# Decay scans with a reset row in PSUM, a dense load of w, four shared PSUM banks and a new issue table, in a gated-recurrence and spatial-gating kernel

## The chip, the cores and the metric

The kernel runs on one core of one Trainium2 chip. The metric is the device time in microseconds (us) of one execution. The time before is 393.78 us, the median of three runs (393.39 to 418.01).

## The reference

Two stages follow each other. The first is a linear recurrence per batch (4) and head (8) over 768 steps with 48 channels: a 48 x 48 state is decayed by w and gets k v^T added at each step, and r reads it together with a bonus term u*k*v^T. The second is a gated feed-forward layer whose gate mixes the 768 positions.

```python
for t in range(S):
    cur = einsum(u * k[t], v[t])
    y[t] = einsum(r[t], state + cur)
    state = w[t][:, None] * state + einsum(k[t], v[t])
h = maximum(x @ w_in, 0)            # x is y, heads side by side: 768 x 384 a batch; d_ff = 1024
u, v = halves of h                  # 512 columns each
v_n = (v - mean) / sqrt(var + 1e-6)
v_s = w_spatial @ v_n + b_spatial
out = (u * v_s) @ w_out
```

All numbers are fp32. The inputs w lie between 0.8 and 0.95.

## The kernel before

The recurrence is done in chunks of 128 steps: 4 batches x 6 chunks, 24 chunks or slots. In a slot the channels of two heads lie on 112 partitions (48, a pad of 16, 48), and four such pairs lie side by side, so that a tile is 112 x (4 x 128).

- `slot_load` (L343) issues five loads on the SyncE queue: W (decays, 129 columns a group with a leading zero), kk (k), rr (r), N (r and k with steps on partitions) and v.
- `slot_prep` (L358) first lets ScalarE check that no w exceeds 1 (L379 or L383, a Relu of w - 1 with a sum into `over`). VectorE then runs two `tensor_tensor_scan`s: L387 forms F, the products of w from a step to the end of the chunk, with the reset ones in the constant row `zr`; L368 forms the running products from the start, in place in W, with 1/Wc as reset value (L390, L392; Wc is the product over the chunk) in the constant row `zf`. kk is multiplied by F (L394) and rr by W (L396). L400 to L403 form the diagonal dg of the bonus term, and L415 (GpSimd) or L420 (ScalarE, four multiplies a tile) put it on a diagonal tile As.
- `slot_a` (L434) multiplies kk and rr on TensorE into two PSUM tiles pa, and L439 copies their upper triangles into As. `slot_kt` (L451, L455) transposes kk by way of a PSUM tile pt into KT. `slot_s` (L505 to L521) makes the state's increment pd, and the state S, Sd. `slot_y` (L470) sums the slot's output in the PSUM tile py.
- `slot_x` splits py into a rounded part and a rest (hi, lo) for three-pass matmuls: L534 casts hi on ScalarE; for the first eight slots L537 subtracts it on TensorE and L540 casts lo on ScalarE.
- `hv_unit`, `g_unit` and `out_unit` are the second stage; their matmuls (ph, pu, pv, po) stand at L547 to L549.

`split64`, `prep_sp` and their kin split the weights into hi and lo at the start, on the vector engines, between the first slots.

PSUM has 8 banks. Before, `psM` has four (tag "pm": ph, pu, pv, po and the filler tile pw), and `psA` one each for A0, A1 (the two pa), py and pt (which pd uses too).

Every piece of work is recorded as an op with the engines that may do it, and the table `PLAN` gives each op an engine and a place; `issue` emits the ops sorted by that place, so that the table alone sets the order on every engine. `fill` goes along TensorE's part of the table and puts matmuls of zeros (`warm`, L748, tile pw) where the table leaves it a gap of over 0.3, up to the sixth slot:

```python
if t < last.start and o.start - t > GAP:
    warm((o.start - t - 0.1) / (0.214 if t > first else 0.43))
```

These fillers are instructions in TensorE's stream like any other. If a value of w is over 1 or a chunk's product is too small, `range_check` sets a flag and `general` does the whole work in another way; the given inputs do not come to that.

Of the kernel before, what the change touches and what calls it, by code (L numbers as in the profile page):

```python
# [8 lines left out]
F32 = mybir.dt.float32  # L9
# [7 lines left out]
C = 128  # L17
# [11 lines left out]
T0 S1s S19u Sv6 A14s V1af V1fu V1jh A1tg V28j Snk Ax7 V2cb V2gb V2rx A2tx V2vr S1mi A1wk V2b5 V2tu V2xo A2zo  # L29
V330 S0 S3b Sb6 S53 S84 A7d V7d Vct Vdc Vim Vaw Vr8 Vdt Vfh Vh4 Af8 Aip Gm1 Ttr Vx6 Vzo Tdf Ag2 Tzt T134  # L30
A16i T18h A19o S12r A1ce V34x V36i V3ad A3ev V3o7 Sgh Aq4 V1le V1mn V1uc A20o V3tk S1x6 A2ip V3d9 V3q4 V3x1
A3z2 V40v S5mh A5tl V5xc S1jh A1s1 G5hi S1qk A1ya G5qr S1l0 A1v5 G55w S5u8 A68z G7hj S18b A1ff V7cf S5z2
A669 V7pi S595 A5v0 V706 S71v A78z V7r1 S7kh A7tx V7wz S7e5 A7le V7ny S7po A7wr V7yi S2u0 A32m V3ca V3s1
V3vi A3x6 G4dl S3cg A3m7 V5ps V64f V6db A6i9 G72o S2zr A38d V5tj V5yw V60j A62p G6ll S3z4 A4lt V71p V77k
V7aw A7eq V7kb T2c7 T31i T37h A3nm A3pw A3qk Scx Seq Srm Skj S9n An1 Vnt Vup Vz7 V11o Vv5 V18i Vt5 Gx2 V1ck
Ahj A1gu A1l6 T1b1 V1ok V1rk Ti6 Vm1 Gzw A17u A13a Txo Az9 T1r7 T1u6 T1vh A22e T24d A2dd T2fc T33g T39f A3c0
A3eb A3tu Ste Sz8 S10z S1eo S16t A10r V153 G1f5 V1tk V1zo G1bl V26m G1ok G1ri V233 A1e3 A24p A291 T295 V2i8
V2dh T11e V1bl G1hr A1zp A23q T1fv V1hr T2ku T2m5 T2ng A2s4 T2u3 A2vn T2xm T2zk T35j A39s A3gk A3h8 A3wd
G4pl V4tu V4ue G4y9 G4zi G505 V52m A55f A57s V5do A536 A5d9 V5nu A5jn A5lz V623 S1cw S1hp S217 S24r S1vn
A1pi V1w9 G2ag V2fh V2zl G233 V38f G2dh G2i8 V2l8 A2kf A2mt G2q5 T3bn V3f2 V3h3 T1k3 V1ql G2l2 A2wz A2r5  # L40
T27c A2ep T3hp T3jp T3l0 A40s T4dy A4gv T4kc T4ma T4o8 A4xm A50x A59h S28p S2c3 S2px S2mw S2rp A2g6 V2mq
V362 V3ee V3ks G3ee V3yy G3hy V42s V44g A2ys A48o G4bt T426 V4g4 V4e4 T2hk V2q5 G44c A45x A4ji T3n8 V4ce
T4ir T4qg T4rr A4vb T4xi A51h T5g7 T5i5 T5k3 A5no A5pz A5qm S3aj S3fh S3n4 S46w S3l6 A3jo V45y V4bd V4bx
V4j8 V49g V4rx G4ge V4mn V4oa A3t0 A4pv G4q5 T4ug V4y9 V532 T4er V4i5 G4o6 A4wn A4uc T53d T566 T57h A5bx
T5dw A5ib T5qt T5sr T5up A5xb A5zl A609 A644 V640 V65y G69t G6cr G6ev G6iu G6jh V6rt A6tm V75n A6o9 A6ql
V7m1 A6k7 A6mk G6v8 T6p4 T3qq T3xk T458 A47c T76b T77s T7dk T7f1 T7ot T7qs V7sw V7vf A7y6 G81m T3tk T3w4
T485 A4d0 T6py T6re T6su T798 T83v T85b V88r V8aj A8c6 V8dp T3z0 T40g T46p A4kh T71z T73f T74v T7ao T7s8
T7to V81m G84e A893 V8f8 T49l T4b1 T4ch A4i7 T6ua T6vq T6x7 T7c4 T7z1 T80h V84o V877 A8ai V8c2 T8jt T8l9
T8tz T8vf A8xi S8z0 T8o6 T8pm T8r2 T8si A8um S8xb T8fh T8gx T8id T8mq A8ot S8qb T5m1 T5zt T6fs A6sa T86r
T888 T89o T8b4 T8ck T8e0 V8gs G8j4 A8m3 V8vd T619 T62p T646 A67o T8wv T8yb T92o T9a4 T9bk Tacp Vaet Gakp  # L50
# [154 lines left out]
def kernel(  # L205
# [670 lines left out]
```

## Time and profile before

| what | us |
|---|---|
| median of three runs | 393.78 |
| the profiled execution's own time | 393.65 |
| its span, first to last instruction | 391.8 |
| around the span | 1.85 |
| TensorE busy in the span | 377.2 |
| VectorE, ScalarE, GpSimd busy | 276.8, 200.0, 142.1 |
| fillers (pw), all before 94.5 | 32.8 |
| last matmul ends | about 385.5 |

The profile is of one execution. Busy time is the union of an engine's instructions; TensorE's matmuls are pipelined, so the ends of two that follow each other overlap. An fp32 matmul (pw, pa, py, pd) shows as two records, one fp32r matmul (L547 to L549) as one. An engine's idle time is put down to what released it last.

### The profile page before, as it was taken

What the parts mean: (1) busy time and instruction counts of PE and PEld (TensorE: products, weight loads), DVE (VectorE), ACT (ScalarE), POOL (GpSimd) and SP (SyncE); (2) the same over time, 40 slices, a digit from 0 to 9 for tenths busy, and PEclk for the clock granted to TensorE, in tenths of its full rate; (3) what the DMA queues carried; (4) which work ended last, traced back from release to release, by engine and by line L of the source; (5) the groups of instructions that cost most, each with busy time, mean ns of one, the idle gap of its engine ahead of it and who ended that gap; (6) DMA issues with size and microseconds to landing.
All of it is one profiled execution on the core that took longest, in us unless ns stands there. A gap on an engine that the chain in (4) does not pass through costs nothing.

```text
span 391.8 us, 9107 instructions
## 1 busy us (share of the span) xinstructions
PE 377.2 (96%) x3638; PEld 342.4 (87%) x3638; DVE 276.8 (71%) x466; ACT 200.0 (51%) x511; POOL 142.1 (36%) x172
## 2 busy tenths in 40 slices
PE   7899989899999999999999999999999999999993
PEld 6788778788899988989988988899988899999993
DVE  5688978869878687878977978995688714414140
ACT  4477675879455457565356256574145604521211
POOL 3248406549433464534431126416343103021110
PEclk9999999999999999999999999999999999999997
DMA  7996562662332545243067434243041110001101
GB/s 233 299 311 195 164 198 64 194 195 57 100 99 84 148 119 154 93 138 96 1 176 197 114 106 135 84 127 107 2 146 40 37 62 0 2 20 40 63 2 69
DMA packets 23091, 43.79 MB, mean 112 GB/s; under 512 B 2688, under 2 KB 10496, under 8 KB 23040
## 3 DMA queue, kind: packets, MB, share of 16 engines
q1 hardware_dynamic: 23040, 43.12, 36.9%
q8 instruction: 30, 0.49, 0.5%
q14 instruction: 21, 0.17, 0.1%
HBM read 38.39 MB, written 4.72 MB: 110 GB/s over the span
## 4 chain that ended last, share of the span: by engine, by line
PE 73%; DMA 9%; DVE 8%; issue 3%; ACT 2%; POOL 2%; SPq 1%; POOLq 0%; ACTq 0%; DVEq 0%
PE pv L547 9%; PE pv L549 8%; PE pv L548 8%; PE py L470 7%; PE pa L434 4%; PE po L547 4%; PE po L549 4%; PE po L548 4%; PE pu L547 4%; PE pu L548 4%; PE pu L549 3%; PE ph L547 3%; PE ph L549 3%; PE ph L548 3%; DMA W<-in_tr_dram 3%
## 5 line engine op out<-in xcount | busy, mean ns | idle before, releaser
L547 PE MATMUL pv<-ws,vh 128*128 128x384 f32 x192 | 66.3, 345 | 0.1
L549 PE MATMUL pv<-ws,vl 128*128 128x384 f32 x192 | 64.6, 337 | 0.0
L548 PE MATMUL pv<-ws,vh 128*128 128x384 f32 x192 | 64.6, 336 | 0.0
L657 ACT CAST gh<-t 128x384 fp32r<-128x384 f32 x32 | 16.1, 510 | 55.5 <-POOL t L655 27.7
L439 DVE COPY_PREDICATED As<-mask,pa 128x512 f32<-128x512 int32 x48 | 34.0, 731 | 9.4 <-PE pa L434 4.7
L547 PEld LDWEIGHTS pv<-ws,vh 128*128 128x128 f32 x192 | 36.1, 188 | 1.9 <-issue 0.4
L415 POOL TENSOR_SCALAR_AFFINE_SELECT As<-dg 128x512 f32<-128x512 f32 x26 | 21.8, 843 | 41.3 <-DVE dg L403 26.4
L387 DVE TENSOR_TENSOR_SCAN F<-W,zr 112x516 f32<-112x516 f32 x24 | 32.2, 1343 | 6.2 <-ACT F L383 3.6
L548 PEld LDWEIGHTS pv<-ws,vh 128*128 128x128 f32 x192 | 36.1, 188 | 0.2
L549 PEld LDWEIGHTS pv<-ws,vl 128*128 128x128 f32 x192 | 36.1, 188 | 0.0
L420 ACT ACTIVATE As<-ident,dg 128x128 f32<-128x128 f32 x88 | 27.9, 391 | 14.4 <-DVE dg L403 11.6
L547 PE MATMUL pu<-xT,wi 128*128 128x384 f32 x96 | 33.8, 352 | 1.4 <-ACT ph L579 1.4
L748 PE MATMUL pw<-zr 128*128 128x128 f32 x228 | 32.8, 292 | 1.7 <-DVE zr L250 1.7
L653 DVE TENSOR_TENSOR t<-pv,b_sb 128x384 f32<-128x384 f32 x32 | 17.5, 552 | 23.6 <-PE pv L549 23.6
L547 PE MATMUL po<-wo,gh 128*128 128x384 f32 x96 | 33.0, 344 | 0.0
L748 PEld LDWEIGHTS pw<-zr 128*128 128x128 f32 x228 | 29.8, 202 | 3.3 <-DVE zr L250 1.7
L548 PE MATMUL pu<-xT,wi 128*128 128x384 f32 x96 | 32.5, 338 | 0.0
L549 PE MATMUL po<-wo,gl 128*128 128x384 f32 x96 | 32.3, 337 | 0.0
L549 PE MATMUL pu<-xT,wi 128*128 128x384 f32 x96 | 32.3, 337 | 0.0
L548 PE MATMUL po<-wo,gh 128*128 128x384 f32 x96 | 32.3, 337 | 0.0
L368 DVE TENSOR_TENSOR_SCAN W<-W,zf 112x516 f32<-112x516 f32 x24 | 32.0, 1333 | 0.3
L547 PE MATMUL ph<-wi,xT 128*128 128x512 f32 x72 | 29.7, 412 | 0.0
(175 smaller groups left out, 878.0 us busy)
## 6 DMA issues: line engine op xcount, KB each, us to landing
N<-in_nat_dram SPq DMA_DIRECT2D x24, 384.0 KB, 3.4
W<-in_tr_dram SPq DMA_DIRECT2D x24, 226.2 KB, 3.2
kk<-in_tr_dram SPq DMA_DIRECT2D x24, 224.0 KB, 2.8
rr<-in_tr_dram SPq DMA_DIRECT2D x24, 224.0 KB, 3.7
v<-in_nat_dram SPq DMA_DIRECT2D x24, 192.0 KB, 2.5
out_dram<-ot SPq DMA_DIRECT2D x24, 192.0 KB, 1.9
wst<-in_w_spT_dram SPq DMA_DIRECT2D x12, 192.0 KB, 3.5
d_('wu', 1)_167<-in_w_in_dram SPq DMA_DIRECT2D x1, 512.0 KB, 7.2
```

The costliest lines, as they stand in the source:

```text
L368: nc.vector.tensor_tensor_scan(E, E, zf[:, :NW], 0.0, ALU.mult, ALU.add)
L387: op({"V": 1.23}, lambda: nc.vector.tensor_tensor_scan(F()[:, ::-1], W()[:, NW:0:-1], zr[:, NW:0:-1], 0.0, ALU.mult, ALU.max), r=[(W, 0)], ...
L415: e.affine_select(out=As(), in_=dg()[:, j::2].unsqueeze(2).broadcast_to([P, G, C]), pattern=[[0, G], [1, C]], compare_op=ALU.is_equal, fil ...
L420: e.mul(As()[:, g, :], ident, dg()[:, 2 * g + j:2 * g + j + 1])
L439: op({"V": 0.725}, lambda j=j, As=As: nc.vector.copy_predicated(As(), mask.unsqueeze(1).broadcast_to([P, G, C]), pa[j]()), r=[(pa[j], 0)], ...
L470: nc.tensor.matmul(py()[Q * n:Q * (n + 1), k_, :], a, b, start=n not in started, stop=not left[0], skip_group_check=True)
L547: nc.tensor.matmul(ps, ah, bh, start=first, stop=False)
L548: nc.tensor.matmul(ps, ah, bl, start=False, stop=False)
L549: nc.tensor.matmul(ps, al, bh, start=False, stop=last)
L653: op({"V": dve(HT)}, lambda: nc.vector.tensor_tensor(t1(), pv()[:, :HT], b_sb[:, tsl], ALU.add), r=[(pv, 0), ("b", 0)], w=[(t1, 0)])
L657: op({"A": act(HT)}, lambda: nc.scalar.copy(gh(), t1()), r=[(t1, 0)], w=[(gh, 0)])
L748: nc.tensor.matmul(pw()[:, :C], zk[:, 1:C + 1], zk[:, 1:C + 1], start=True, stop=True)
```

## The change

Both scans now read the reset values as first operand from zz, a tile of 4 x 128 in a PSUM bank of its own, and combine by max and then multiply: a column of ones at the end of each group, and at its start 0 for the backward scan and 1/Wc for the forward scan. A ScalarE copy (L403) sets the start column back to 0 after each slot. The forward scan writes its result E into the PSUM bank of pa_0, and not over W; since it stands one step later, the first column of rr is multiplied by 1/Wc apart (L401).

W is loaded as a dense 112 x (4 x 128) tile, from a source whose rows of 128 are 129 apart. The check of w leaves the slots: `check_w` loads all of w once more in 16 loads of 128 x 768 into the buffer of N, and ScalarE runs a Relu with a sum on each (L376). pt and pd take their tiles from the four banks of `psM`, and pw moves into the unused fourth part of the bank of py. The table is new. TensorE's cost in the table is slightly higher for the three-pass matmuls.

```diff
 PLAN = """
-T0 S1s S19u Sv6 A14s V1af V1fu V1jh A1tg V28j Snk Ax7 V2cb V2gb V2rx A2tx V2vr S1mi A1wk V2b5 V2tu V2xo A2zo
+T0 S9g S1tc S12t A1hk V1q0 V1vu V1zp A21p V23j Ss6 A11w V146 V18s V1cw A1fv G1ic S1hh A1rs V1up V25g V2e6
...
+    psX = ctx.enter_context(tc.tile_pool(name="psX", bufs=1, space=bass.MemoryType.PSUM))
...
+    zz = psX.tile([P, G, C], F32, name="zz")
+    nc.vector.memset(zz, 0.0)
+    nc.vector.memset(zz[:, :, C - 1:], 1.0)
+
+    pyw = psX.tile([P, KX + 1, C], F32, name="pyw")
+    pw = pyw[:, KX, :]
...
-        load(W, [0], lambda: nc.sync.dma_start(W(), tr[b, c, :, :WE]), R * WE * 4)
+        load(W, [0], lambda: nc.sync.dma_start(
+            W(), tr[b, c, :, 1:WE].rearrange("p (g t) -> p g t", t=C + 1)[:, :, :C]), R * G * C * 4)
...
+    def check_w(n):
+        w = buf(p2, [P, 2, DM], "N", f"Nw{n}", 1)
...
+        load(w, [0], lambda: nc.sync.dma_start(flat(), gt[n, :, 0, :]), P * S * 4)
+        op({"A": 1.03}, lambda: nc.scalar.activation(flat(), flat(), AF.Relu, bias=neg, accum_out=over[:, n:n + 1]),
+           r=[(w, 0)], w=[(w, 0), ("over", n)])
...
-            op({"A": 0.91}, lambda: nc.scalar.activation(
-                F()[:, :NW], W()[:, 1:], AF.Relu, bias=neg, accum_out=over[:, i:i + 1]),
-               r=[(W, 0)], w=[(F, 0), ("over", i)])
...
-        op({"V": 1.23}, lambda: nc.vector.tensor_tensor_scan(
-            F()[:, ::-1], W()[:, NW:0:-1], zr[:, NW:0:-1], 0.0, ALU.mult, ALU.max), r=[(W, 0)], w=[(F, 0)], port=True)
+        op({"V": 1.24}, lambda: nc.vector.tensor_tensor_scan(
+            flat(F()[:R])[:, ::-1], flat(zz[:R])[:, ::-1], flat(W())[:, ::-1], 0.0, ALU.max, ALU.mult),
+           r=[(W, 0), ("zz", 0)], w=[(F, 0)])
...
+        op({"V": 0.17}, lambda: nc.vector.reciprocal(zz[:R, :, 0], Wc), r=[("Wc", i)], w=[("zz", 0)])
+
+        op({"V": 1.24}, lambda: nc.vector.tensor_tensor_scan(
+            flat(E()[:R]), flat(zz[:R]), flat(W()), 0.0, ALU.max, ALU.mult), r=[(W, 0), ("zz", 0)], w=[(E, 0)])
+        op({"V": 0.17}, lambda: nc.vector.tensor_tensor(rr()[:, :, 0], rr()[:, :, 0], zz[:R, :, 0], ALU.mult),
+           r=[("zz", 0)], w=[(rr, 1)])
+        op({"A": 0.2}, lambda: nc.scalar.copy(zz[:R, :, 0], zk[:R, :G]), r=[("zz", 0)], w=[("zz", 0)])
...
-        pt = buf(psA, [P, G, R], "pt", f"pt{i}", 1)
+        pm_ = buf(psM, [P, 512], "pm", f"pt{i}", 4)
...
+        py.make = lambda: pyw[:, :KX, :]
...
-        pd = buf(psA, [P, G, D], "pt", f"pd{i}", 1)
+        pm_ = buf(psM, [P, 512], "pm", f"pd{i}", 4)
...
-            nc.tensor.matmul(pw()[:, :C], zk[:, 1:C + 1], zk[:, 1:C + 1], start=True, stop=True)
+            nc.tensor.matmul(pw, zk, zk, start=False, stop=True, skip_group_check=True)
```

The new table moves nearly every instruction. Three places follow. The first is TensorE in the second slot. Before, from the second half of the first slot's py on; pw are fillers, and of pa, pt, pd and py the first row of each stands here:

```order
L470 MATMUL py_258<-As_1_194,v_136 32x128 [waits DVE_49]
L748 MATMUL pw<-zr 128x128 x6
L537 MATMUL py_258<-xT_0_0_296,nident 128x384 [waits Activation_49]
L748 MATMUL pw<-zr 128x128 x2
L434 MATMUL pa_0_317<-rr_206,kk_161 128x128 [waits DVE_49]
L451 MATMUL pt_343<-ident,kk_252 128x112 [waits DVE_49,Pool_49]
L748 MATMUL pw<-zr 128x128 x5
L505 MATMUL pd_366<-v_298,KT_356 64x48 [waits DMAHW2_49,DVE_49]
L748 MATMUL pw<-zr 128x128 x9
L470 MATMUL py_402<-As_0_348,v_138 32x128 [waits DVE_49]
```

Now, from the subtraction for the first slot on (L554 is L537 of before, L444 L434, L464 L451, L484 L470, L763 L748); pyw is the bank that py and the fillers share:

```order
L554 MATMUL pyw<-xT_0_0_263,nident 128x384
L763 MATMUL pyw<-zk 128x128 x2
L444 MATMUL pa_0_246<-rr_154,kk_140 128x128 [waits DMAHW1_49,DVE_49,PE_49]
L763 MATMUL pyw<-zk 128x128 [waits Activation_49]
L763 MATMUL pyw<-zk 128x128 x12
L484 MATMUL pyw<-As_0_306,v_152 32x128 [waits DVE_49]
L763 MATMUL pyw<-zk 128x128 x7
L464 MATMUL pt_373<-ident,kk_218 128x112 [waits DMAHW4_49,Pool_49]
L763 MATMUL pyw<-zk 128x128 x2
L484 MATMUL pyw<-As_1_324,v_152 32x128 [waits DVE_49]
```

Before, no filler waits for another engine after the first one of all. Now a group of 13 begins with one that waits for ScalarE: for the cast of lo (L557) that reads py in the same bank. Over the whole program the fillers fall from 114 to 82, and six of the 17 groups begin with such a wait.

The second place is ScalarE up to that cast. Before, from the check of the third W to the cast of lo for the first slot (L540):

```order
L383 ACTIVATE F_268,over<-W_209,neg 112x516 [waits DMAHW5_49,DVE_49]
L521 COPY Sd<-S_103 48x4x48 [waits Pool_49]
L321 ACTIVATE e_('wv', 0)_293<-d_('wv', 0)_239 128x512 [waits DMAHW6_49]
L534 CAST xT_0_0_296<-py_258 128x3x128 [waits PE_49]
L521 COPY Sd<-S_103 48x4x48
L540 CAST xT_0_1_311<-py_258 128x3x128 [waits PE_49]
```

Now, from the cast of hi (L551) to that of lo (L557):

```order
L551 CAST xT_0_0_263<-pyw 128x3x128 [waits PE_49]
L538 COPY Sd<-S_108 48x4x48 [waits Pool_49]
L403 COPY zz<-zk 112x4 [waits DVE_49]
L329 ACTIVATE e_('wv', 1)_287<-d_('wv', 1)_221 128x512 [waits DMAHW5_49]
L304 CAST ws_117<-wst_1_256 128x384 [waits DMAHW6_49]
L430 ACTIVATE As_0_306<-ident,dg_300 128x128 [waits DVE_49]
L430 ACTIVATE As_0_306<-ident,dg_300 128x128 x3
L417 COPY vp_111<-v_278 128x4x2x16 [waits DMAHW0_49,Activation_49]
L557 CAST xT_0_1_319<-pyw 128x3x128 [waits PE_49]
```

Before, one copy stood between the two casts; now a weight's multiply, a weight's cast and the four multiplies of a diagonal tile stand there too.

The third place is VectorE in the first slot. Before, from the first scan to the product rr that the first pa needs:

```order
L387 SCALAR_TENSOR_TENSOR F_134<-W_125,zr 112x516 [waits DMAHW0_49,DVE_49]
L271 CAST mask<-mneg 128x128 [waits Pool_49]
L394 TENSOR_TENSOR kk_128<-kk_128,F_134 112x512 [waits DMAHW2_49,DVE_49]
L390 TENSOR_SCALAR prod<-F_134 112x4
L392 RECIPROCAL zf<-prod 112x4 [waits DVE_49]
L400 TENSOR_TENSOR N_130<-N_130 128x384 [waits DMAHW3_49]
L402 TENSOR_TENSOR N_130<-N_130,u_sb 128x384 [waits DMAHW1_49,DVE_49]
L403 TENSOR_REDUCE dg_169<-N_130 128x8 [waits DVE_49]
L368 SCALAR_TENSOR_TENSOR W_125<-W_125,zf 112x516 [waits Activation_49]
L511 COPY S_102<-pd_177 112x192 [waits PE_49]
L387 SCALAR_TENSOR_TENSOR F_201<-W_144,zr 112x516 [waits DMAHW7_49]
L396 TENSOR_TENSOR rr_141<-rr_141,W_125 112x512 [waits DMAHW6_49,DVE_49]
```

Now the same stretch (L391 and L399 are the scans, L406 the product):

```order
L391 SCALAR_TENSOR_TENSOR F_137<-zz,W_129 112x512 [waits DMAHW0_49,DVE_49]
L280 CAST mask<-mneg 128x128 [waits Pool_49]
L395 TENSOR_SCALAR prod<-F_137 112x4 [waits DVE_49]
L397 RECIPROCAL zz<-prod 112x4 [waits DVE_49]
L399 SCALAR_TENSOR_TENSOR pa_0_150<-zz,W_129 112x512 [waits DVE_49]
L406 TENSOR_TENSOR rr_135<-rr_135,pa_0_150 112x4x127 [waits DMAHW3_49,DVE_49]
```

The products kk and N of this slot are now GpSimd's, and nothing of the next slot stands ahead of rr.

## Rows read from the trace of the kernel before

**Rows 1.** The page: busy time by engine, and TensorE's granted clock in 40 slices.
```profile
PE 377.2 (96%) x3638; PEld 342.4 (87%) x3638; DVE 276.8 (71%) x466; ACT 200.0 (51%) x511; POOL 142.1 (36%) x172
...
PEclk9999999999999999999999999999999999999997
```

**Rows 2.** Busy time by stretch: us, PE, PEld, DVE, ACT, POOL, clock, DMA share, GB/s.
```profile
0.00:20.00 20.00, 15.78 (x164) 14.20 (x164) 12.94 (x23) 9.15 (x22) 5.93 (x18) 1.00 0.92 267
20.00:60.00 40.00, 37.89 (x441) 32.61 (x442) 35.20 (x56) 28.17 (x77) 17.54 (x15) 1.00 0.68 210
60.00:100.00 40.00, 38.95 (x400) 33.48 (x401) 33.64 (x54) 30.89 (x77) 26.88 (x29) 1.00 0.45 132
100.00:385.60 285.60, 284.56 (x2635) 262.13 (x2634) 195.02 (x336) 131.31 (x337) 91.78 (x113) 1.00 0.29 85
385.60:391.80 6.20, 0.00 (x0) 0.00 (x0) 0.00 (x0) 0.47 (x1) 0.00 (x0) 0.67 0.26 89
```

**Rows 3.** The same for the fillers (tile pw) alone: PE, PEld, clock, DMA.
```profile
0.00:60.00 60.00, 27.79 (x192) 25.21 (x192) 1.00 0.76 229
...
sum 100.00, PE 32.82 PEld 29.82; mean PE 16.41 PEld 14.91
```

**Rows 4.** The chain that ended last, around 21 us: start, us, what.
```profile
20.85 0.44 PE pw L748 x4
```

**Rows 5.** Timeline of TensorE: start, us, line, records. The first pa.
```profile
12.75 1.16 PE L434 MATMUL pa<-rr,kk 48*128 48x128 f32 x16
```

**Rows 6.** Timeline of VectorE: scans, the mask and the first rr.
```profile
3.90 1.23 DVE L387 TENSOR_TENSOR_SCAN F<-W,zr 112x516 f32<-112x516 f32 x1 [2.29 <-DMA W<-in_tr_dram]
5.05 0.20 DVE L271 CAST mask<-mneg 128x128 int32<-128x128 f32 x1
...
11.35 0.67 DVE L396 TENSOR_TENSOR rr<-rr,W 112x512 f32<-112x512 f32 x1
...
27.81 2.03 DVE L387 TENSOR_TENSOR_SCAN F<-W,zr 112x516 f32<-112x516 f32 x1
```

**Rows 7.** Timeline of GpSimd beside that last scan.
```profile
28.83 1.80 POOL L402 TENSOR_TENSOR N<-N,u_sb 128x384 f32<-128x384 f32 x1
```

**Rows 8.** By line: ns min/median/max of the first scan and of an addition from PSUM.
```profile
L387 DVE TENSOR_TENSOR_SCAN F<-W,zr x24: 1203/1230/2032, 3.9 to 295.8; 112x516 f32<-112x516 f32 x24
...
L653 DVE TENSOR_TENSOR t<-pv,b_sb x32: 532/554/559, 109.1 to 379.2; 128x384 f32<-128x384 f32 x32
```

**Rows 9.** Groups: out<-in, shapes, count | busy, mean ns | idle before, releasers.
```profile
L387 DVE TENSOR_TENSOR_SCAN F<-W,zr 112x516 f32<-112x516 f32 x24 | 32.2, 1343 | 6.2 <-ACT F L383 3.6 <-DMA W<-in_tr_dram 2.6
...
L383 ACT ACTIVATE F<-W,neg 112x516 f32<-112x516 f32 x22 | 15.9, 724 | 12.7 <-DMA W<-in_tr_dram 8.9 <-issue 2.1 <-POOL prod L390 1.0
...
L392 DVE RECIPROCAL zf<-prod 112x4 f32<-112x4 f32 x24 | 4.2, 174 | 0.7
```

**Rows 10.** Timeline of TensorE and ScalarE: subtractions (L537), casts of lo (L540), diagonal multiplies (L420).
```profile
20.40 0.45 PE L537 MATMUL py<-xT,nident 128*128 128x384 f32 x1 [1.04 <-ACT xT L534]
...
20.89 0.48 ACT L540 CAST xT<-py 128x384 fp32r<-128x384 f32 x1 [0.28 <-PE py L537]
...
32.70 0.44 PE L537 MATMUL py<-xT,nident 128*128 128x384 f32 x1 [0.26 <-ACT xT L534]
...
33.05 2.45 ACT L420 ACTIVATE As<-ident,dg 128x128 f32<-128x128 f32 x8
...
35.41 0.45 ACT L540 CAST xT<-py 128x384 fp32r<-128x384 f32 x1
```

**Rows 11.** DMA: packets, MB, share of 16 engines; then loads, KB each, us to landing.
```profile
q1 hardware_dynamic: 23040, 43.12, 36.9%
...
W<-in_tr_dram SPq DMA_DIRECT2D x24, 226.2 KB, 3.2
kk<-in_tr_dram SPq DMA_DIRECT2D x24, 224.0 KB, 2.8
```

**Rows 12.** Waits: us in total, times, longest. TensorE's longest for a common bank.
```profile
PE pu L547 <- ACT ph L579: 1.4, 1, 1.4
```

More of the change, by code (lines that the diff above doesn't have):

```diff
@@ L34 @@
[L34 to L38, printed above, removed]
@@ L285 @@
     NS = B * NC_
-    NW = WE - 1
-    over = cp.tile([R, NS], F32, name="over")
+    over = cp.tile([P, B * G], F32, name="over")
     prod = cp.tile([R, NS, G], F32, name="prod")
@@ L374, in slot_prep @@
-        if i == 0:
-            for j in range(2):
-                st[j]["junk"] = buf(psA, [P, G, C], f"A{j}", f"over{j}", 1)
-        if i < 2:
-            t = q["junk"]
-            op({"A": 0.88}, lambda: nc.scalar.activation(
-                t()[:R], W()[:, 1:].rearrange("p (g t) -> p g t", t=C + 1)[:, :, :C], AF.Relu, bias=neg,
-                accum_out=over[:, i:i + 1]), r=[(W, 0)], w=[(t, 0), ("over", i)])
-        else:
-            op({"A": 0.91}, lambda: nc.scalar.activation(
-                F()[:, :NW], W()[:, 1:], AF.Relu, bias=neg, accum_out=over[:, i:i + 1]),
-               r=[(W, 0)], w=[(F, 0), ("over", i)])
@@ L426, in slot_a @@
         kk, rr = q["kk"], q["rr"]
-        pa = [buf(psA, [P, G, C], f"A{j}", f"pa{i}_{j}", 1) for j in range(2)]
+        pa = [q["pa"], buf(psA, [P, G, C], "A1", f"pa{i}_1", 1)]
         def mm():
@@ L762, in range_check @@
         bad = cp.tile([1, 1], I32, name="bad")
-        pk = buf(psA, [P, 512], "py", "pk", 1)
+        pk = buf(psA, [P, C], "py", "pk", 1)
+        pk.make = lambda: pyw[:, 0, :]
         def low():
             nc.vector.tensor_scalar(over, over, 0.0, None, ALU.is_le)
-            nc.vector.tensor_reduce(okr[:, 0:1], over, AX.X, ALU.min)
+            nc.vector.tensor_reduce(okr[:, 0:1], over[:R], AX.X, ALU.min)
             nc.vector.tensor_scalar(prod, prod, FLOOR, None, ALU.is_gt)
@@ L770, in low @@
             nc.vector.tensor_tensor(okr[:, 0:1], okr[:, 0:1], okr[:, 1:2], ALU.min)
-        op({"V": 0.9}, low, r=[("over", i) for i in range(NS)] + [("Wc", i) for i in range(NS)] + [("S1",)],
+        op({"V": 0.9}, low, r=[("over", i) for i in range(B * G)] + [("Wc", i) for i in range(NS)] + [("S1",)],
            w=[("okr",)] + [("Wc", i) for i in range(NS)])
@@ L804 @@
         if i == FILL_TO:
-            prog.last = last = op({"T": 0.1}, lambda: warm(1), r=[(vn[0, c][0], 0)], w=[(pw, 0)])
+            prog.last = last = op({"T": 0.1}, lambda: warm(1), r=[(vn[0, c][0], 0)], w=[("pw", 0)])
         if c == NC_ - 1:
+            for g in range(G):
+                check_w(b * G + g)
             for h in range(2):
```

243 lines of the change are left out of this document (124 added, 119 removed).

## The prediction

> **What bounds the kernel now.** I read the page first, then the table of stretches, then the same table for the fillers alone, then the timelines of the first 40 us. The page has TensorE busy for 96% of the span, at full clock in every slice but the last [rows 1]. The stretches say where this is real [rows 2]: from 100 us to 385.6 TensorE is idle for 1.0 us in 285.6, and the last 6.2 us are the final copy and store. Nothing in the change takes a matmul of the second stage away, so these two stretches, 291.8 us, can only be kept or spoiled. The first 100 us are another matter. TensorE is busy for 15.78 + 37.89 + 38.95 = 92.6 us there, but 32.8 of these are fillers [rows 3], so 59.8 us are work and 40.2 us are fillers or idle (7.4 us). What can be won lies in these 40.2 us, most of it before 60 us (27.8 us of fillers). There TensorE waits for slots to be prepared, and VectorE is the fullest of those that prepare: 48.1 of the first 60 us, against 37.3 on ScalarE and 23.5 on GpSimd, with the DMA engines at a share of 0.92 in the first 20 us [rows 2].
>
> **What the change takes off the preparation.** The scans: the first has a median of 1230 ns, a worst of 2032 [rows 8] and a mean of 1343 [rows 9]. The slow ones stand beside GpSimd work, as the one of 2.03 us beside a product of 1.80 [rows 6, 7]. The nearest row with an operand in PSUM, the addition L653, stays between 532 and 559 ns in all 32 [rows 8], so I take the new scans, which read zz from PSUM, at 1.23 each: 48 x 0.11 = 5.3 us less on VectorE. The new multiply of rr's first column comes 24 times and costs 0.174 each by the reciprocal of the same size [rows 9], 4.2 us. So the scans alone give VectorE nothing much; its relief is in the products that the table hands to GpSimd.
>
> The check: a Relu of 724 ns stood ahead of the backward scan in 22 slots, and the scans waited 3.6 us for them in all [rows 9]. Sixteen checks of 768 columns replace 24; at 724 ns for 516 columns one is 1.08 us, 17 against 17 us in sum, on an engine that is half idle, and the loads that they need come after those of the early slots. These loads, 6.3 MB, go where the DMA share is 0.45 and 0.29 [rows 2]. I cost both at nothing; what a scan waits for next is its W, or the reset of zz in (e).
>
> The order: in the first slot rr comes fifth after the first scan on VectorE instead of eleventh. From the scan's start at 3.90: 1.23 scan, 0.2 mask [rows 6], 0.17 and 0.17 for prod and reciprocal, 1.23 scan, 0.67 product make 7.6, against 12.0 before (11.35 + 0.67). If rr has landed, the first pa starts at 8.3 or so and not at 12.75 [rows 5]: 4.4 us earlier. Later slots can gain a little more, as no scan pair is held at 2 us again.
>
> **The sum.** (a) Fillers. The order has 32 fewer, 82 for 114. Two of them back to back take 0.44 us on the chain [rows 4], 0.22 each: -7.0. Over all 114 the mean is 32.8/114 = 0.29, which gives -9.2, and that is the other end. The table puts fillers where it sees TensorE wait, so their number is only the table's opinion; that the first pa can come 4.4 us earlier is the second source for a gain of this size. If no slot is ready sooner, the term is 0.
>
> (b) The new waits of fillers. A filler used to wait for nobody. Now it writes the bank of py, and six groups begin with one that waits until ScalarE has cast py. All that stands behind it in TensorE's stream waits too: the next slot's py, pt, pd, and through them KT and the state on ScalarE and VectorE. The price of such a wait shows in the casts of before: the cast of lo ended 0.52 us after the first subtraction (20.89 + 0.48 - 20.85), but 2.7 us after the second (35.86 - 33.14), with eight diagonal multiplies of 2.45 us in front of it [rows 10]. With four groups at the first price and two at the second, 2.1 + 5.4 = 7.5 us is the upper end; 0 is the lower, where TensorE would have waited anyway. Between subtraction and fillers now stand two fillers and a pa (0.44 + 1.1), which leaves 1.2 of 2.7 for the group of 13; with 0.8 for the other five, which have pd or pt in between, I take +2.0.
>
> (c) W in short pieces. A row of W was one piece of 2 KB; now it is four of 512 bytes, 448 a load and 28 an engine. The mean piece takes 36.9% x 391.8 x 16 / 23040 = 0.10 us for 1.87 KB [rows 11]. In proportion to bytes nothing changes; with 0.10 us a piece whatever its size, a load takes 2.8 us of each engine instead of 0.7, 2.1 more. Three loads of W fall into the first 20 us with their DMA share of 0.92 [rows 2]: 0 to +6.3. Packets are likelier to go by bytes than by count, as W and kk with rows of 2 KB land alike at 3.2 and 2.8 us; I take 0.2 a load, +0.6. The Trainium skill, page "DMA: Bandwidth & Descriptors", section "Specifications", gives 512 bytes as the smallest transfer that still runs at line rate, which is just the size here; by it this term is 0 and the sum 389.1. No row here shows a piece of 512 bytes.
>
> (d) Banks. pt and pd (40 tiles) leave a bank of their own for the four in which ph, pu, pv and po (112 tiles) turn over. After 100 us TensorE lost 1.0 us in all with these; at that rate 40 more cost 0.4, which I take. The one long wait for a bank was 1.4 us [rows 12]; if every fourth of the 40 met one, it would be 14.
>
> (e) The forward scan writes the bank of pa_0, so it waits for the slot before to be copied out; the backward scan waits for ScalarE's reset of zz, where it waited for the check. One for one, 0, with 3.6 us [rows 9] on either side.
>
> Sum: -7.0 + 2.0 + 0.6 + 0.4 = -4.0 on the execution's own 393.65 gives **389.7 us** (the median of the runs lies 0.13 higher). A difference of 2%, 7.9 us, is about what a measurement of this kernel can tell from no change.
>
> **Rivals.** *The whole gain arrives.* The casts are over before the fillers come up, fillers count at 0.29, and (c) and (d) are 0: 393.65 - 9.2 = 384.5. For it: ScalarE has time, 37 of 60 us. Against: the cast stands behind four diagonal multiplies that need dg, and so the N load and two products on GpSimd.
>
> *Nothing is gained: the loads set the early slots.* DMA runs at 0.92 at first and the first scan waited for its W [rows 6]. Then fewer fillers only mean more idle time, and the time is 393.5. Against: rr is now fourth in the load queue, before it was seventh, and the bytes before the third slot are the same.
>
> *The fillers' waits eat more than is won.* Place: the six groups before 60 us. Price: 7.5 us as in (b), and, as two casts of lo now also wait for fillers that stand after the subtraction, another 0.4 + 1.3 (two and six fillers at 0.22): 9.3. Then -7.0 + 9.3 + 1.0 = +3.3, 397.0 us. It decides from waits of 6.0 us on. For it: TensorE's stream is in order, and each lost piece also delays KT, and so the next cast. Against: part of the wait falls where py's own operand As is late anyway.
>
> **Chances.** The forecast (386.9 to 392) has 0.46, the whole gain 0.22, nothing gained 0.17, the waits 0.15. The range 384.5 to 397.0 leaves out half of the second and a bit under half of the last, 0.18. Faster by over 2% (under 385.9) holds most of the second case: 0.17. Slower by over 2% (over 401.7) needs the last case, or the banks of (d) at their worst: 0.05. Within: 0.78.
>
> **What would show it.** Right: 164 filler records instead of 228; the first pa near 8 to 9 us; scans with a mean of 1.23 to 1.25; in the list of waits, fillers behind the casts for about 2 us; TensorE's work of the first stage done about 4 us earlier, and the stretch after 100 us with no more than 1.5 us idle. Wrong: filler waits of over 5 us; loads of W that land much later than those of kk; pt, pd or pv waiting for banks after 100 us; scans that still reach 2 us.

## The result, and the profile after

| what | before | after |
|---|---|---|
| median, us (20 runs each) | 393.93 | 391.48 (389.02 to 392.95) |
| the profiled execution | 393.65 | 390.85 |
| its span | 391.8 | 389.1 |
| last matmul ends | 385.5 | 383.0 |

The ratio to the kernel before is 0.9937 (95% interval 0.9919 to 0.9956): 0.6% faster, within the 2% called no difference in the prediction. Repeated beside the experiments it was 0.9984 (0.9967 to 1.0002). The two intervals do not overlap, so from one group of runs to another a ratio can move by about half a percent (1.8 us), more than its interval allows for; differences of 2 us between groups need a trace, or a second pair of runs, beside them. The forecast was a gain of 4.0 us, to 389.7 for the profiled execution. Measured were 2.8 us there and 2.4 in the medians, and 0.6 in the repeat: 1.2 to 3.4 us of the expected gain are missing.

The page after answers to [rows 1]. One slice of the granted clock is no longer at full speed:

```profile
PE 370.6 (95%) x3574; PEld 337.1 (87%) x3574; DVE 254.8 (65%) x466; ACT 202.3 (52%) x533; POOL 150.9 (39%) x207
...
PEclk9969999999999999999999999999999999999998
```

The stretches, to be held against [rows 2] (columns as there):

```profile
0.00:20.00 20.00, 13.63 (x151) 11.86 (x152) 13.82 (x26) 9.77 (x27) 10.56 (x25) 0.96 0.95 290
20.00:60.00 40.00, 37.21 (x428) 32.58 (x428) 29.92 (x50) 22.93 (x62) 20.12 (x25) 0.93 0.69 209
60.00:100.00 40.00, 39.43 (x349) 36.02 (x349) 30.91 (x60) 31.11 (x77) 21.61 (x28) 1.00 0.49 144
100.00:383.00 283.00, 280.31 (x2655) 256.64 (x2653) 180.16 (x333) 138.01 (x370) 98.64 (x132) 1.00 0.36 105
383.00:389.10 6.10, 0.03 (x1) 0.00 (x0) 0.00 (x0) 0.48 (x1) 0.00 (x0) 0.84 0.21 75
```

And the fillers (L763) alone, against [rows 3]:

```profile
0.00:60.00 60.00, 24.64 (x152) 22.39 (x152) 0.94 0.78 236
60.00:100.00 40.00, 1.76 (x12) 1.55 (x12) 1.00 0.49 144
sum 100.00, PE 26.40 PEld 23.94; mean PE 13.20 PEld 11.97
```

The reader can now add up where the span went. Fillers: 32.8 to 26.4, -6.4. TensorE idle before 100 us: 100 - 92.6 = 7.4 before, 100 - 90.3 = 9.7 now, +2.3. Idle from 100 us to the last matmul: 285.5 - 284.5 = 1.0 before, 283.0 - 280.3 = 2.7 now, +1.7. Matmuls that are work: 344.3 and 344.2, -0.1; the tail: 6.3 and 6.1, -0.2. Sum -2.7, from 391.8 to 389.1.

TensorE's timeline shows the second slot. The first pa comes at 8.54, 4.2 us earlier than in [rows 5], and the second at 15.46. Then there are 2.92 us of idle time, and 13 fillers (26 records) that take 5.9 us:

```profile
8.54 1.16 PE L444 MATMUL pa<-rr,kk 48*128 48x128 f32 x16 [0.19 <-DVE rr L401]
...
15.46 1.16 PE L444 MATMUL pa<-rr,kk 48*128 48x128 f32 x16
19.55 5.92 PE L763 MATMUL pyw<-zk 128*128 128x128 f32 x26 [2.92 <-ACT xT L557]
25.39 0.43 PE L484 MATMUL pyw<-As,v 128*32 128x128 f32 x8
```

ScalarE's timeline says why the cast of lo (L557) was late, though the subtraction that it needs had ended at 15.1: it stood behind a weight's multiply, which waited 0.95 us for its load, a weight's cast, four diagonal multiplies and the copy of v of the third slot, which waited 0.94 us for its load. The last two of these, and the cast:

```profile
16.60 1.27 ACT L430 ACTIVATE As<-ident,dg 128x128 f32<-128x128 f32 x4
18.82 0.30 ACT L417 COPY vp<-v 128x128 f32<-128x128 f32 x1 [0.94 <-DMA v<-in_nat_dram]
19.02 0.47 ACT L557 CAST xT<-pyw 128x384 fp32r<-128x384 f32 x1
```

And the stretches around it show why 13 fillers took 0.45 us each and not 0.22: the granted clock (the number before the DMA share) stood at 0.50, the lower of the two levels, 1.2 GHz.

```profile
16.60:19.50 2.90, 0.02 (x2) 0.00 (x0) 1.36 (x2) 1.96 (x8) 0.05 (x1) 0.83 1.05 323
19.50:25.40 5.90, 5.86 (x28) 5.63 (x28) 4.95 (x8) 2.52 (x7) 4.80 (x6) 0.50 1.06 328
25.40:30.00 4.60, 4.60 (x86) 4.08 (x87) 0.57 (x2) 1.13 (x2) 2.17 (x3) 1.00 0.24 85
```

TensorE's waits, of which the first and third are fillers behind casts (us in total, times, longest), and the scans (ns min/median/max) against [rows 8]:

```profile
PE pyw L763 <- ACT xT L557: 4.1, 3, 2.9
PE pyw L763 <- DVE zz L259: 1.9, 1, 1.9
PE pyw L763 <- ACT xT L551: 1.8, 2, 1.1
...
PE pt L464 <- ACT ph L596: 0.5, 1, 0.5
```
```profile
L391 DVE TENSOR_TENSOR_SCAN F<-zz,W x24: 1193/1217/1224, 4.0 to 286.9; 112x512 f32<-112x512 f32 x24
```

No scan is stretched any more: the longest of the first is 1.224 us, of the second (L399) 1.248. W lands like kk:

```profile
W<-in_tr_dram SPq DMA_DIRECT2D x24, 224.0 KB, 3.1
kk<-in_tr_dram SPq DMA_DIRECT2D x24, 224.0 KB, 2.9
```

Last, the chain that ended last has a piece that did not exist before: the loads of the check (Nw) and its Relus (L376), one after the other, each load waiting until the Relu before it has left the buffer.

```profile
150.78 4.55 DMA Nw<-in_gt_dram
...
155.44 1.03 ACT Nw L376 x2
...
156.49 3.58 DMA Nw<-in_gt_dram
...
160.16 1.04 ACT Nw L376 x2
...
167.29 0.82 ACT ph L596 x2
```

The Relus as a group (columns as in [rows 9], where the old check stands) waited 15.7 us for these loads, and ScalarE's other work stood behind them:

```profile
L376 ACT ACTIVATE Nw<-Nw,neg 128x768 f32<-128x768 f32 x16 | 15.0, 935 | 15.7 <-DMA Nw<-in_gt_dram 15.7
```

TensorE's longest wait after 100 us is of another kind. pd waits for the slot's v, whose load was issued at 151.22, 0.44 us behind the check's load at 150.78, and took 4.7 us to land:

```profile
156.04 0.64 PE L522 MATMUL pd<-v,KT 128*64 128x48 f32 x16 [0.81 <-DMA v<-in_nat_dram]
```

### The profile page after: what moved, and what is told of

It is laid out like the page before. It is cut to its first block, busy times and chain, and to the rows that moved or that the text cites. A ratio compares the mean times of both kernels' runs of the same rounds, so it can differ in the third digit from the quotient of the medians.

```text
span 389.1 us, 9089 instructions
## 1 busy us (share of the span) xinstructions
PE 370.6 (95%) x3574; PEld 337.1 (87%) x3574; DVE 254.8 (65%) x466; ACT 202.3 (52%) x533; POOL 150.9 (39%) x207
## 4 chain that ended last, share of the span: by engine, by line
PE 79%; DMA 9%; DVE 3%; ACT 3%; issue 2%; POOL 2%; SPq 0%; ACTq 0%; DVEq 0%; POOLq 0%
PE pv L564 8%; PE pyw L484 8%; PE pv L566 8%; PE pv L565 8%; PE pa L444 5%; PE pyw L763 5%; DMA Nw<-in_gt_dram 4%; PE po L564 4%; PE pu L564 4%; PE po L566 4%; PE po L565 4%; PE pu L566 4%; PE pu L565 3%; PE ph L564 3%; PE ph L565 3%; PE ph L566 3%
## 5 line engine op out<-in xcount | busy, mean ns | idle before, releaser
L430 ACT ACTIVATE As<-ident,dg 128x128 f32<-128x128 f32 x120 | 38.0, 390 | 13.5 <-DVE dg L413 12.9
L449 DVE COPY_PREDICATED As<-mask,pa 128x512 f32<-128x512 int32 x48 | 34.9, 746 | 8.0 <-POOL As L425 2.8
L670 DVE TENSOR_TENSOR t<-pv,b_sb 128x384 f32<-128x384 f32 x32 | 17.8, 555 | 31.0 <-PE pv L566 30.6
L675 POOL TENSOR_TENSOR gl<-t,gh 128x384 fp32r<-128x384 f32 x17 | 18.3, 1076 | 41.8 <-ACT gh L674 41.8
L763 PE MATMUL pyw<-zk 128*128 128x128 f32 x164 | 26.4, 318 | 7.7 <-ACT xT L557 4.1
L391 DVE TENSOR_TENSOR_SCAN F<-zz,W 112x512 f32<-112x512 f32 x24 | 29.2, 1216 | 6.3 <-DMA W<-in_tr_dram 4.5
L763 PEld LDWEIGHTS pyw<-zk 128*128 128x128 f32 x164 | 23.9, 226 | 9.6 <-ACT xT L557 4.8
L399 DVE TENSOR_TENSOR_SCAN pa<-zz,W 112x512 f32<-112x512 f32 x24 | 29.5, 1228 | 0.5
```

What stands on the lines that cost most here:

```text
L391: op({"V": 1.24}, lambda: nc.vector.tensor_tensor_scan(flat(F()[:R])[:, ::-1], flat(zz[:R])[:, ::-1], flat(W())[:, ::-1], 0.0, ALU.max, AL ...
L399: op({"V": 1.24}, lambda: nc.vector.tensor_tensor_scan(flat(E()[:R]), flat(zz[:R]), flat(W()), 0.0, ALU.max, ALU.mult), r=[(W, 0), ("zz", ...
L430: e.mul(As()[:, g, :], ident, dg()[:, 2 * g + j:2 * g + j + 1])
L449: op({"V": 0.725}, lambda j=j, As=As: nc.vector.copy_predicated(As(), mask.unsqueeze(1).broadcast_to([P, G, C]), pa[j]()), r=[(pa[j], 0)], ...
L670: op({"V": dve(HT)}, lambda: nc.vector.tensor_tensor(t1(), pv()[:, :HT], b_sb[:, tsl], ALU.add), r=[(pv, 0), ("b", 0)], w=[(t1, 0)])
L675: op({"G": pool(HT), "V": dve(HT)}, lambda e: e.tensor_tensor(gl(), t1(), gh().bitcast(F32), ALU.subtract), r=[(t1, 0), (gh, 0)], w=[(gl, ...
```

## The experiments

They ran in three groups of four, each beside the kernel before (medians 392.71, 392.16 and 392.65). "Ratio" is to that. Number 5 ran in the second group, so its distance to 1 to 4 and to 9 to 12 is one between groups, and distances in us are between medians unless ratios are named. A trace shows one execution, and not always a typical one: those of numbers 1 and 5 took 2.4 and 2.6 us less than their kernel's median, those of 2 and 4 2.1 and 1.9 us more. Theory A: the fillers' waits, and the clock behind the long one, gave back what the first slots won. Rival B: the loads set the early slots. Rival C: waits for a PSUM bank. Rival D: the check of w.

**1. Fillers in a common bank.**

```diff
-    pw = pyw[:, KX, :]
+    pw = buf(psM, [P, 512], "pm", "pw", 4)
```

> The fillers write a tile of the four common banks again, as before the change, so that none of them waits for a cast; all else is the changed kernel. Theory A (the one long wait, and TensorE's clock after it, gave back what the first slots won): after the first subtraction and the second pa, at 16.6 us, the 13 fillers start at once and at full clock, 2.9 us instead of 2.9 us of wait and 5.84 us of work; the second slot's py starts when its As is copied, near 20.6 us instead of 25.39; no stretch in 10 to 40 us with a granted clock under 0.9; time 391.5 - 4.8 = 386.7 us, 386 to 388.5. Rival B (the loads set the early slots, which take 3 us and more beside one another): py as before or the third slot late by as much, time 391 to 392. Rival C (one bank less for ph, pt and pd until the fillers end makes new waits): waits of pt, pd or ph for a bank appear, time over 391.5.

Median 393.15, ratio 1.0019 (0.9991 to 1.0046): not faster than the changed kernel, if anything slower. In the trace the fillers indeed ran at once, and the seventh pa started at 71.3 us instead of 74.4. But the next pa came at 108.9 instead of 108.6. Between them TensorE waited for a bank three times, as the last filler kept one of the four until 87.7 us:

```profile
79.26 0.44 PE L562 MATMUL pu<-xT,wi 128*128 128x384 f32 x1 [1.38 <-ACT ph L594]
82.74 0.44 PE L562 MATMUL pu<-xT,wi 128*128 128x384 f32 x1 [0.58 <-ACT us L659]
86.72 0.44 PE L562 MATMUL pv<-ws,vh 128*128 128x384 f32 x1 [0.58 <-ACT us L659]
```

So the experiment changed two things: a wait went, and a bank. Number 6 parts them.

**2. The cast of lo earlier.** One word of the table: `A1a7` becomes `A11i`.

> Only ScalarE's order is changed, in one place: the cast of lo of the first slot stands right after the two copies into Sd, ahead of a weight's multiply, a weight's cast, four diagonal multiplies and the copy of the third slot's v. The fillers stay in the bank of py. Theory A: the cast runs at 15.1 us, when the subtraction ends, and not at 19.02, so the 13 fillers follow the second pa without a wait and at full clock; the other five groups keep their waits (0.78 + 1.06 + 0.57 us and less). Time 387 to 389 us. Rival B: 391 to 392. Against e1 it tells the long wait from the shared bank as such: if the five short waits matter, this one is 1 to 2.4 us above e1, if not the same.

Median 392.67, ratio 0.9983 (0.9948 to 1.0018): that of the changed kernel in number 5, so theory A's gain does not come in the median. The traced execution took 394.73 us at a mean granted clock of 0.981; four of the twelve took 389.5 to 390.4 us at 0.988 to 0.994, so what follows is not in every execution alike. The long wait is gone from the trace (second slot's py at 21.54), but a new one stands 8 us on. TensorE idles 2.05 us before the third pa, since VectorE has the product rr (L406) behind a weight's work (L331) that waits, by way of ScalarE, for a load, which is rival B in another form: a load that delays a slot it does not belong to; the granted clock then stays at 0.50 from 30 to 43.5 us, in its first part:

```profile
26.18 0.67 ACT L329 ACTIVATE e_('wu', 2)_399<-d_('wu', 2)_353 128x512 f32<-128x512 f32 x1 [1.23 <-DMA d_('wu', 2)_353<-in_w_in_dram]
```
```profile
26.89 1.04 DVE L331 TENSOR_SCALAR e_('wu', 2)_399<-e_('wu', 2)_399 128x512 int32<-128x512 int32 x1 [0.47 <-ACT e_('wu', 2)_399 L329]
27.85 1.22 DVE L331 TENSOR_SCALAR e_('wv', 0)_363<-e_('wv', 0)_363 128x512 int32<-128x512 int32 x1
28.99 0.67 DVE L406 TENSOR_TENSOR rr<-rr,pa 112x508 f32<-112x508 f32 x1
```
```profile
30.00:36.00 6.00, 4.94 (x34) 4.15 (x33) 4.43 (x9) 2.76 (x6) 2.93 (x1) 0.50 0.56 156
36.00:42.00 6.00, 5.43 (x30) 4.48 (x28) 4.24 (x8) 3.36 (x9) 3.71 (x4) 0.50 0.66 227
```

**3. Without the group of 13.**

```diff
-                if t < last.start and o.start - t > GAP:
+                if t < last.start and o.start - t > GAP and o.n != 173:
```

> The group of 13 fillers alone is left out. The cast of lo still comes at 19 us and the second slot's py, which uses the same bank, still has to wait for it. Theory A in two parts: if what costs is mostly the 13 fillers run at the low clock in front of py, py now starts near 20.6 us (its As), still at the low clock for a while, and the time is 387.5 to 389; the distance to e1 is then what the low clock costs on the work behind it. If it is the idle time itself (2.9 us, now longer) that counts, the time stays at 391 to 392. Rival B: 391 to 392.

Median 391.96, ratio 0.9986 (0.9963 to 1.0009): no gain. The second slot's py started at 22.39 and not at 20.6, after 4.68 us of idle time, with the clock at 0.50 until about 27. So the group stood mostly in time that was lost anyway: the triangle that py multiplies (As) was late too.

**4. No check.** The 16 loads and Relus are not issued, and `over` is filled with zeros.

> The check of w is left out: its 16 loads of 128 x 768 and ScalarE's 16 Relus are not issued. Rival D (the new check, whose loads take the buffer of N in turn with the slots and whose Relus stand in ScalarE's order, makes the 2.7 us that TensorE is now idle after 100 us, 1.0 before): idle after 100 us back to 1.0, time 389.8 us. Theory A: the loss lies before 60 us; time 390.8 to 391.8.

Median 388.77, ratio 0.9901 (0.9872 to 0.9929): 2.8 us below the changed kernel's median in number 5; by the ratios 1.4 or 3.3 us, as one takes its 0.9937 or its 0.9984; numbers 2 and 3, which ran beside this one, stand with 0.9983 and 0.9986 at the second. Idle from 100 us to the last matmul (at 382.7) is 0.4 us, where the changed kernel has 2.7 and, in number 5, 1.6. Neither pd's wait for v nor pt's for a bank is left there. The early stage was no better (seventh pa at 77.0):

```profile
100.00:382.70 282.70, 282.28 (x2670) 259.36 (x2669) 182.53 (x336) 128.92 (x348) 100.16 (x134) 1.00 0.30 88
```

Rival D holds, and in time is larger than the 1.7 us it said; in idle time after 100 us it is 1.2 to 2.3 us.

**5. The changed kernel again.**

> The changed kernel itself, beside the others on one chip. If its gain of 0.63% is a property of the kernel, 390.2 us where the kernel before has 392.7, and its second trace shows the idle time of 2.9 us before the 13 fillers and a granted clock near 0.5 after it again. If the early stage differs from one execution to the next (third pa at 29.8 to 34.0 us in the five traces so far), the low stretch stands elsewhere or is shorter, and the start of the seventh pa differs from 74.4 us by 2 us or more.

Median 391.56, ratio 0.9984 (0.9967 to 1.0002). The wait before the 13 fillers is there again (2.5 us), the third pa came at 30.6 and the seventh at 73.5, and idle time after 100 us was 1.6 us where it had been 2.7. A single trace is thus good for a microsecond or two here, no better.

**6. The fillers' bank freed at their end.** As 1, and the last filler is not issued.

```diff
-            prog.last = last = op({"T": 0.1}, lambda: warm(1), r=[(vn[0, c][0], 0)], w=[(pw, 0)])
+            prog.last = last = op({"T": 0.1}, lambda: None, r=[(vn[0, c][0], 0)], w=[("pw", 0)])
```

> As the first experiment (fillers in a common bank), but the very last filler, which stood at 87 us and held that bank until then, is not issued; the bank is free from about 63.6 us. Rival C of before, as its trace now has it (the bank that fillers hold makes pu and pv wait 1.38 + 0.58 + 0.58 us between 79 and 87): these three waits go, and with the seventh pa at 71 us the time is 2.5 us below that experiment's, 390 to 391 in the median. If the gain of the first slots is lost for another reason between 71 and 109 us, other waits stand there and the time stays at 393.

Median 389.58, ratio 0.9941 (0.992 to 0.9961): 2.0 us below number 5, and by the ratios 3.1 below number 1. The three waits for a bank are gone, rival C's point; one more, of pd, stands at 48.5 us (2.0 us), where the fillers still hold their bank. No filler waits for a cast, but the second slot's py still waits 2.08 us, until 22.25. This py waits in the program for VectorE alone (the list of waits names ScalarE's L428, which ended at the same moment, for the slot's other tile). VectorE had copied its triangle (L447) only behind the third slot's scan, which waited for W:

```profile
19.65 1.22 DVE L389 TENSOR_TENSOR_SCAN F<-zz,W 112x512 f32<-112x512 f32 x1 [0.89 <-DMA W<-in_tr_dram]
20.79 0.67 DVE L330 SCALAR_TENSOR_TENSOR e_('wv', 1)_287<-d_('wv', 1)_221,e_('wv', 1)_287 128x512 int32<-128x512 int32 x1
21.38 0.73 DVE L447 COPY_PREDICATED As<-mask,pa 128x512 f32<-128x512 int32 x1
```

So the fillers' place is worth 2.0 us, not 4.8, because a wait for a load stands right behind it.

**7. A buffer of its own for the check.** The tag "N" of `check_w` becomes "Nw".

> The loads of the check get a buffer of their own and no longer take turns with the slots' N; no instruction is added or moved. Leaving the check out took the idle time of TensorE after 100 us from 2.7 to 0.4 us. Theory D1 (the shared buffer makes the loads wait in turn, and SyncE's queue behind them): idle after 100 us falls to 1 us or less, time 1.5 us below the changed kernel's. Theory D2 (ScalarE's order: a Relu that waits for its load holds up what stands behind it): the idle time stays above 2 us, time as the changed kernel's, within 0.7 us.

Median 390.39, ratio 0.9951 (0.9925 to 0.9977), 1.2 us below number 5, but the intervals overlap, and the idle time after 100 us is 1.6 us as in number 5. By the recorded text D1 needed 1 us or less and D2 more than 2, so it decides for neither. The wait of pd for v is still there (0.80 us), and so is one of pt behind a Relu (0.2 us): loads beside one another and ScalarE's order both outlive the shared buffer.

**8. The kernel before, with fillers in py's bank.** This one part of the change alone.

> The kernel before with this one part of the change: the fillers write the unused fourth part of the bank of py. Nine of its filler groups now begin with a wait for ScalarE. Theory A (such waits, and the clock after the longer ones, cost the early stage): waits of fillers of 2 to 6 us in sum, the seventh pa later than 80.7 us by 1 to 4, time 394 to 397 us where the kernel before has 392.7. If they only stand where TensorE would have waited anyway, the time is 392 to 393.5 and the seventh pa within 0.7 us of 80.7.

Median 399.37, ratio 1.0174 (1.0139 to 1.0208): 6.8 us slower, more than theory A said. The seventh pa starts at 87.4 instead of 80.7, and the waits are the fillers':

```profile
PE pyw L752 <- ACT xT L539: 5.7, 3, 2.5
PE pyw L752 <- ACT xT L545: 2.5, 3, 1.3
```

**9. Both repairs (6 and 7) together.**

> The changed kernel with two repairs together: the fillers in a common bank that is freed at their end, and a buffer of its own for the loads of the check. Alone they stood at 0.9941 and 0.9951 of the kernel before, the changed kernel beside them at 0.9984. If the first costs the stage before 100 us and the second the stage after it, they add: 0.9984 - 0.0043 - 0.0033 = 0.991, 388.5 us where the kernel before has 392.2; idle time of TensorE after 100 us under 1.5 us. If one covers what the other gains, 0.994 and 389.6 us.

Median 387.76, ratio 0.9867 (0.9828 to 0.9906): below number 6 by 1.8 us (2.9 by the ratios), with intervals that don't overlap, and 1.1 us idle after 100 us where number 6 has 1.8. Number 10, which ran beside it and is the changed kernel but for W's layout, is 3.5 us above. So the two add, and it is likely that the shared buffer (D1) carries a part of the check's price; how large a part these runs don't fix. In this trace too pd waits 0.7 us for v.

**10. W in whole rows.** The host stores w densely, so a row of W is one piece of 2 KB.

> The changed kernel with w stored so that a row of W is one piece of 2 KB and not four of 512 bytes; nothing else. If the short pieces cost DMA time in proportion to their number (2.1 us an engine and load at the worst), the loads of W in the first 30 us land earlier (5.2 to 5.7 us from issue now), the third slot's scan starts 1 to 2 us before 18.1 us and the time is 1 to 4 us lower. If they go by bytes, the landing of W stays within 0.5 us of kk's and the time within 0.3% of the changed kernel's.

Median 391.25, ratio 0.9966 (0.9946 to 0.9986), 0.3 us from number 5; W landed in 3.0 us, kk in 2.9, in the first 40 us in 5.1 and 4.5 (5.7 and 4.8 in number 5). The short pieces cost nothing that shows. The Trainium skill, page "DMA: Bandwidth & Descriptors", section "Specifications", gives 512 bytes as the smallest transfer that still runs at line rate. This run agrees.

**11. zz in SBUF, and a fifth common bank.**

```diff
-    zz = psX.tile([P, G, C], F32, name="zz")
+    zz = cp.tile([P, G, C], F32, name="zz")
```

> The changed kernel with zz in SBUF instead of PSUM, and the bank that this frees as a fifth common bank. Two things are read apart in the trace. Scans: if the operand in PSUM is what keeps them from being slowed beside GpSimd, their mean goes from 1216 and 1228 ns up to the 1343 of before, with single ones near 2000, and VectorE is busier by 3 to 6 us; if not, it stays under 1240. Banks: if pt and pd in the four common banks cost something, waits of pt, pd and pu for a bank (0.5 + 0.4 us in the list now) go, and TensorE's idle time after 100 us falls by that, 0.5 to 1 us. Time: 0 to 1 us below the changed kernel's by the banks, 0 to 3 above it by the scans.

Median 400.86, ratio 1.0187 (1.0145 to 1.023), 9.3 us above number 5 (8.0 by the ratios) and far outside the expectation, in spite of a bank more. The scans are stretched again, one to 3.6 us, and GpSimd is slower too (170.3 us busy for 150.9, with the same instructions). So is the small product of rr's first column with zz (L401), 13.2 us in all where it took 4 (0.16 us each). TensorE's idle time after 100 us is 7.4 us for 2.7:

```profile
PE 372.1 (93%) x3574; PEld 337.6 (85%) x3574; DVE 271.2 (68%) x466; ACT 202.8 (51%) x533; POOL 170.3 (43%) x207
```
```profile
L391 DVE TENSOR_TENSOR_SCAN F<-zz,W x24: 1196/1233/2058, 3.9 to 296.2; 112x512 f32<-112x512 f32 x24
```
```profile
L399 DVE TENSOR_TENSOR_SCAN pa<-zz,W x24: 1215/1232/3556, 5.6 to 299.2; 112x512 f32<-112x512 f32 x24
```
```profile
L401 DVE TENSOR_TENSOR rr<-rr,zz 112x4 f32<-112x4 f32 x24 | 13.2, 548 | 10.8 <-DMA rr<-in_tr_dram 10.6
```

The Trainium skill, page "SBUF — State Buffer", section "Who interferes with whom", has it that a VectorE instruction with two inputs in SBUF contends with a GpSimd instruction that reads SBUF, and one with at most one such input, outside the modes that use two ports, doesn't. By these rows the trace agrees.

**12. Both repairs, and four places of the first slots' order.** Four words of the table: `A1a7`, `V1ap`, `V15c`, `V1r6` become `A11i`, `V19u`, `V1ao`, `V1ke`.

> As the run with both repairs, and in four places the order of the first slots is changed so that nothing that can be done stands behind a wait for the loads of the third and fourth slot: VectorE copies the second slot's triangle ahead of the third slot's first scan and multiplies the third rr ahead of the fourth slot's first scan; ScalarE casts lo of the first slot ahead of a weight's multiply, a weight's cast and the copy of the third slot's v. Rival B in its new form (the loads, which run at a DMA share above 1.0 from 10 to 30 us, set the early slots through these waits in order): the second slot's py starts near 19 us and not at 22 to 25, the third pa 1 to 3 us before 30.6 us, the seventh before 72, time 1 to 3 us below the run with both repairs. If the third slot's own loads set it, the third pa stays at 30 to 31 us and the time with it.

Median 385.8, ratio 0.9811 (0.9781 to 0.984), 2.0 us below number 9, which ran beside it (the intervals overlap a little), and below the kernel before by 1.9%. TensorE's second py, third pa and clock:

```profile
17.01 3.17 PE L763 MATMUL pw<-zk 128*128 128x128 f32 x26
20.20 0.43 PE L482 MATMUL pyw<-As,v 128*32 128x128 f32 x8
...
27.51 1.16 PE L442 MATMUL pa<-rr,kk 48*128 48x128 f32 x16
```
```profile
PEclk9999999999999999999999999999999999999999
```

The third pa starts at 27.5 us where all other kernels with this table have 29.8 to 34.0, the seventh at 69.8. So the loads delayed the early slots through what was queued behind a wait for them, which is rival B in its new form. That no load sets them in any other way is not shown: VectorE still waits 2.9 us for W in the first 60 us (5.4 in number 9).

## Why the prediction was nearly right

**(a) Fillers, -7.0.** Right: 164 records, the first pa at 8.54 (8.3 forecast), and -6.4 us. Without the 2.9 us that 13 fillers lost at the lower clock it would have been -9.3, the other end given: that the middle was met is partly luck, for the prediction had no low clock in it.

**(b) Waits of fillers, +2.0.** The size was right, by luck, and the way to it was not. The waits came to 4.1 + 1.8 = 5.9 us, and the clock behind the longest, which the prediction did not think of, to 2.9 more. By the prediction's own sign (filler waits of over 5 us) the term was wrong, and they were just short of the 6.0 us from which its third rival was to decide. Yet taking them away gained 2.0 us (number 6), since what stood against the third rival was true: part of the wait falls where py's own As is late anyway. What was late next was a load, through VectorE's order, as in the second rival. In the order of before the same edit costs 6.8 us (number 8), near the upper end of 7.5.

**(c) Short pieces, +0.6.** Nothing, by number 10.

**(d) Banks, +0.4.** Two waits of pt, 0.5 + 0.4 us in TensorE's list, and one of 0.6 in number 5. The first is for a bank that ph's ScalarE work (L596) gave back at 168.1, and in the chain above that work stands behind a Relu of the check. Without the check (number 4) neither is left. So the size was met, but what was met is mostly the check's; that the second is for a bank at all is not shown, and no run tried the banks alone.

**(e) The reset of zz, 0.** F waited 1.3 us for it, where it waited 3.6 for the check [rows 9].

**The step that failed** is the check: "I cost both at nothing." Its Relus were not longer than forecast (15.0 us for 17), and neither ScalarE nor the DMA engines were full. What was missed is that both stand in queues: a load that waits for a shared buffer in SyncE's, and a Relu that waits for its load in ScalarE's, 15.7 us in all. And its loads lie beside others: v, issued right behind one, made TensorE wait 0.8 us, though over the stage the DMA engines were at a share of 0.36. Leaving the check out gains 2.8 us (number 4). With it at +2.8 in place of 0 and (c) and (d) at 0 the sum is -7.0 + 2.0 + 2.8 = -2.2; measured were -2.4 and, in the repeat, -0.6.

The other signs that the prediction named came out so. TensorE's work was ahead as forecast: before 100 us it did 90.3 - 26.4 = 63.9 us of it, for 59.8 before, 4.1 us more. The idle time after 100 us was 2.7 us, not at most 1.5.

A second thing was priced far too low, without harm to the sum as it was part of (a): "the scans alone give VectorE nothing much". In the new order the operand in PSUM is worth 8 to 9 us (number 11), as GpSimd's products are shorter with it too.

How much of the check's price is the buffer, how much ScalarE's order and how much its loads beside the others is not settled: the own buffer gave 1.2 us with overlapping intervals (number 7) and 1.8 us on top of number 6 (number 9), and no run moved the Relus or the loads alone.

## What to carry to other kernels

Work that an engine has time for still costs if it waits inside an in-order queue: for each added load or operation ask what it waits for and what stands behind it. When a wait is taken away, read in the same trace what is late next before counting the gain; here one repair gave 0 to 2.0 us (numbers 2, 6 and 7), two together 3.5 and two with the first slots' order 5.5 (numbers 9 and 12, against number 10 beside them). Fillers that are there for TensorE's clock should wait for nobody, and should not keep a bank that others need.

## What was not expected of the hardware

Idle time of TensorE cost twice in the early stage. After idle stretches of 2.92 us (after), 2.05 (number 2), 1.82 (number 1) and 4.68 us (number 3) the granted clock was 0.50 for 3 to 14 us. The length of one stretch does not tell it alone. In number 6 a wait of 2.00 us left the clock at 1.00, through the wait and in the 3.5 us behind it:

```profile
48.53 0.64 PE L520 MATMUL pd<-v,KT 128*64 128x48 f32 x16 [2.00 <-ACT ph L594]
```

And before the same instruction, a wait of 1.06 us was followed by a clock of 1.00 in the changed kernel and of 0.50 in number 3:

```profile
34.30:36.00 1.70, 1.70 (x25) 1.53 (x25) 1.39 (x4) 0.92 (x2) 0.00 (x0) 1.00 1.04 294
```
```profile
34.00:36.00 2.00, 2.00 (x19) 1.78 (x19) 1.85 (x4) 0.64 (x2) 0.17 (x1) 0.50 0.95 263
```

The first row is the changed kernel, the second number 3. The other surprise is number 11's: moving one operand of VectorE's scans, 4 x 128 values a row, from PSUM to SBUF went with GpSimd's work being 13% longer (170.3 for 150.9 us), and with VectorE's product of rr's first column with that operand taking up to 3.04 us for 0.16.
